# Loading batch 1's tokens and batch 2's x behind batch 0's read, and issuing that read's small moves later

## The chip, the cores and the metric

The kernel runs on one core of one Trainium2 chip. The metric is the device time of one execution, in microseconds. Three executions of the kernel before took 503.93, 504.53 and 505.17 us; the median is 504.53 us.

The engines are named as the profile names them: PE is the matrix engine, with PEld for its weight loads; DVE is the vector engine; ACT is the scalar engine; SP is the engine whose queue issues most of the transfers (SPq in the rows).

## The reference

The program is a two-sided attention between 512 positions and 32 state rows, for 8 batches of 8 heads of width 64, followed by four dense products.

```
scores  = scale * x @ state^T;   a  = softmax(scores);   xread = a  @ state
scores2 = scale * state @ x^T;   a2 = softmax(scores2);  sread = a2 @ x
y   = concat(xread, sread) as (8 * 544) rows of 512
out = ((y @ w1) * (y @ w2)) @ w3 @ w_out
```

All data are float32; the weights come as float64 bits and are converted on the chip.

## The kernel before, in words

**The work per batch.** For each batch b the kernel computes the scores from `x_d` (x with the head's width on the partitions) and `st` (the state), takes both softmaxes, and multiplies the state into w1 and w2 (`sw_steps`), so that the first dense products come straight from the attention weights (`stage1_sums`, line 310). Every float32 operand of a large product is split into a high and a low part (`split`, lines 97 and 98: a copy on ACT, a subtraction on DVE), and three products are summed. Batch 0 is handled by `stage1` and `stage2` in the prologue. Batches 1 to 7 are handled by `quarter_batch`, which does the second dense product in a scheme with fewer multiplications; the combined weights that it needs (`t_parts`) are made by `combine_weights(k)`, k = 0 to 3. The calls with k = 0, 1, 2 stand between batch 0's last pieces, the call with k = 3 stands in batch 1's part, behind its second first-stage piece (lines 497 and 498).

**First-stage pieces.** In `quarter_batch` a loop over ft = 0 to 7 runs 12 large matmuls per piece into a pair of PSUM banks (`two_banks`, three such pairs, named ps). ACT copies one bank (line 484) and DVE multiplies it with the other (line 391); after that the pair is free for a later piece. Behind ft = 1 stand, in this order in the program: the state's read of this batch, the score matmuls of the next batch (line 147), the loads for the batches after, and, in batch 1 alone, `combine_weights(3)`: two sums per call on line 363, four differences on line 369, then a split on lines 97 and 98 named t_hi and t_lo. Then the softmax of the next batch goes on, and the pieces ft = 2 to 7 follow. In `stage2_quarters` two pairs of `sw` products of the next batch (line 147, `units` and `more`) stand between the second-stage products (line 418); they use the same three pairs of banks, and DVE frees a pair with the split named sw_lo.

**The state's read (`read_state`).** It needs two things: the batch's tokens (`x_s`, 1 MB, one buffer only) and the second softmax turned into the tile `a2["t"]`. The second comes from DVE's transpose on line 228 into `blocks` (named work) and 16 transfers of 32 KB that regroup the blocks (`move_blocks`, line 171; for batch 0 the rows read work<-work, for the later batches e<-work). The read is 64 small matmuls (line 243), then on DVE a multiplication (line 248, `scaled`) and a transpose (line 252, `turned`, one buffer only), then 16 transfers of 4 KB that put `turned` into `sread` (line 171, sread<-turned). `sread` is used only at the very end, in `state_rows`.

**What sets the order.** The program order holds on PE and on SP, since both are under `manual_schedule`: what is traced first is issued first. DVE and ACT are ordered, behind the prologue, by a planner that walks through the program with estimated costs, and gives an engine, when it is free, the waiting instruction that stands earliest in the program among those whose inputs it takes to be ready; `high_priority` puts line 391's multiplications first. `side_steps` builds the list of pieces that run between batch 0's last products: first three steps of batch 1's softmax, then batch 0's read and two `sw` products, later the rest of batch 1's softmax (`rest`, with line 228 and its 16 transfers), then two more `sw` products.

**The order on SP around the change.** Before: batch 0's 16 sread<-turned transfers, batch 1's 16 e<-work transfers, then, behind the loop over `tt`, `load_tokens(1)` (x_s of batch 1) and `load_x(2)` (st and x_d of batch 2). The single buffer of `x_s` comes free when batch 0's read has ended on PE.

Of the kernel before, what the change touches and what calls it, by code (L numbers as in the profile page):

```python
# [39 lines left out]
def attn_bilinear_kernel(  # L40
# [47 lines left out]
    def bank():  # L88
        return ps_o.tile([P, NF], F32, name="ps_o")

    def two_banks():
        return ps_2.tile([P, 2, NF], F32, name="ps_2")

    def split(hi, lo, src):

        return (
            nc.scalar.copy(out=hi, in_=src),  # L97
            nc.vector.tensor_tensor(out=lo, in0=src, in1=hi.bitcast(F32), op=ALU.subtract),  # L98
        )
# [41 lines left out]
    def per_head(ps, b, moving):  # L141


        for j in range(NP):
            for q in range(KT):
                rows = slice(q * D, (q + 1) * D)
                nc.tensor.matmul(  # L147
                    ps[j * NS:(j + 1) * NS, q], sts[b][rows, j], moving(rows, j), start=True, stop=True
                )

    def load_x(b):
        sts[b] = att.tile([P, NP, NS], F32, name="st")
        nc.sync.dma_start(out=sts[b], in_=st[b])
        x_tiles[b] = att.tile([P, NP, S], F32, name="x_d", bufs=1)
        nc.sync.dma_start(out=x_tiles[b], in_=x_d[b])

    def load_tokens(b):
        token_tiles[b] = att.tile([P, NT, H, D], F32, name="x_s", bufs=1)
        nc.sync.dma_start(out=token_tiles[b], in_=x_s[b])
# [4 lines left out]
    def work_tile():  # L164
        return att.tile([P, KT, S], F32, name="work")

    def move_blocks(dest, src):

        for j in range(NP):
            for c in range(P // NS):  # L170
                nc.sync.dma_start(  # L171
                    out=dest(slice(c * NS, (c + 1) * NS), j), in_=src(slice(j * NS, (j + 1) * NS), c)
                )

    def attention_steps(b):
        xd = x_tiles[b]
        a2 = {}

        def scores():

            ps = two_banks()
            per_head(ps, b, lambda rows, j: xd[rows, j])
            yield
            flat = lambda t: t.rearrange("p k s -> p (k s)")

            s1 = work_tile()
            nc.vector.transpose(out=flat(s1), in_=flat(ps))

            m2 = att.tile([P, KT], F32, name="m2")
            nc.vector.tensor_reduce(out=m2, in_=ps, axis=AX.X, op=ALU.max)  # L190
            nc.vector.tensor_scalar_mul(m2, m2, -SCALE)
            e2 = att.tile([P, KT, S], F32, name="e2", bufs=1)
            sum2 = att.tile([P, KT], F32, name="sum2")
            a2["e"], a2["sum"] = e2, sum2
            for kt in range(KT):
                one = slice(kt, kt + 1)
                nc.scalar.activation(
                    out=e2[:, kt], in_=ps[:, kt], func=AF.Exp, bias=m2[:, one], scale=SCALE, accum_out=sum2[:, one]
                )

            J = KT * S // NS
            s1v = flat(s1).rearrange("p (j n) -> p j n", n=NS)
            m1 = att.tile([P, J], F32, name="m1")
            nc.vector.tensor_reduce(out=m1, in_=s1v, axis=AX.X, op=ALU.max)
            nc.vector.tensor_tensor(
                out=s1v, in0=s1v, in1=m1.unsqueeze(2).broadcast_to([P, J, NS]), op=ALU.subtract
            )
            nc.scalar.activation(out=s1, in_=s1, func=AF.Exp, scale=SCALE)
            yield
            nc.vector.tensor_scalar_add(sum2, sum2, 1e-9)  # L210
            nc.vector.reciprocal(out=sum2, in_=sum2)
            sum1 = att.tile([P, J], F32, name="sum1")
            nc.vector.tensor_reduce(out=sum1, in_=s1v, axis=AX.X, op=ALU.add)
            nc.vector.tensor_scalar_add(sum1, sum1, 1e-9)
            nc.vector.reciprocal(out=sum1, in_=sum1)
            nc.vector.tensor_tensor(
                out=s1v, in0=s1v, in1=sum1.unsqueeze(2).broadcast_to([P, J, NS]), op=ALU.mult
            )
            yield
            at = work_tile()  # L220
            nc.vector.transpose(out=flat(at), in_=flat(s1))
            at_tiles[b] = [att.tile([P, KT, S], F32R, name=f"at_{part}", bufs=1) for part in ("hi", "lo")]
            last = split(*at_tiles[b], at)
            yield

            blocks = work_tile()
            with tc.issue_after(last[1].ins):
                nc.vector.transpose(out=flat(blocks), in_=flat(e2))
            a2["t"] = work_tile() if b < PLAIN else att.tile([P, KT, S], F32, name="e2", bufs=1)
            tiles = lambda t: t.rearrange("p k (t m) -> p (k t) m", m=P)  # L230
            move_blocks(lambda its, j: tiles(a2["t"])[its, :, j * NS:(j + 1) * NS],
                        lambda mine, c: tiles(blocks)[mine, :, c * NS:(c + 1) * NS])

        def read_state():

            xs = token_tiles[b]

            ps = (bank() if b else two_banks()[:, 0])[:, :KT * D].rearrange("p (k d) -> p k d", k=KT)
            for kt in range(KT):
                for t in range(NT):  # L240
                    for j in range(NP):
                        mine = slice(j * NS, (j + 1) * NS)
                        nc.tensor.matmul(  # L243
                            ps[mine, kt], a2["t"][:, kt, t * P + j * NS:t * P + (j + 1) * NS],
                            xs[:, t, 2 * j + kt], start=(t == 0), stop=(t == NT - 1),
                        )
            scaled = att.tile([P, KT, D], F32, name="scaled")
            a2["read"] = nc.vector.tensor_tensor(
                out=scaled, in0=ps, in1=a2["sum"].unsqueeze(2).broadcast_to([P, KT, D]), op=ALU.mult
            )  # L250
            turned = att.tile([P, KT, D], F32, name="turned", bufs=1)
            nc.vector.transpose(
                out=turned.rearrange("p k d -> p (k d)"), in_=scaled.rearrange("p k d -> p (k d)")
            )
            move_blocks(lambda its, j: sread[its, j, b * NS:(b + 1) * NS],
                        lambda mine, c: turned.rearrange("p k (c n) -> p (k c) n", n=NS)[mine, c])

        return scores, read_state, a2


# [80 lines left out]
    reads = {}  # L341

    def side_steps():

        scores, reads[1], _ = attention_steps(1)
        w = sw_steps(1)
        softmax = scores()

        def rest():

            with tc.issue_after(stored[0].ins):
                yield from softmax

        return [[partial(islice, softmax, 3)], [reads[0], w[0], w[1]], [], [rest], [w[2], w[3]], []]

    QF = FT // 2
    HT, HO = S // 2, DO // 2
# [14 lines left out]
    def tmp_tile():  # L372
        return main.tile([P, NF], F32, name="tmp", bufs=4)
# [102 lines left out]
    def quarter_batch(b):  # L476
        q = {"raw": []}
        w = sw_steps(b + 1) if b + 1 < B else [lambda: None] * 4
        softmax = iter(())
        for ft in range(FT):  # L480
            ps = stage1_sums(b, ft)
            a_sb = tmp_tile()
            with tc.high_priority():
                nc.scalar.copy(out=a_sb, in_=ps[:, 0])  # L484
            hidden_quarters(a_sb, ps[:, 1], ft, q)
            if ft == 1:
                reads[b]()
                if b + 1 < B:
                    scores, reads[b + 1], _ = attention_steps(b + 1)
                    softmax = scores()  # L490
                    next(softmax)
                    load_tokens(b + 1)
                if b + 2 < B:
                    load_x(b + 2)
            elif ft in (2, 4):
                next(softmax, None)
            if b == PLAIN and ft == 1:
                combine_weights(QF - 1)
        stage2_quarters(b, q, w[:2], [*w[2:], lambda: softmax])

    def run(steps):
        for step in steps:
            for _ in step() or ():
                pass


    with tc.tile_pool(name="pro", bufs=2) as pro:
# [62 lines left out]
        softmax = scores()  # L570
# [48 lines left out]
    for tt in range(NT):  # L619
# [5 lines left out]
        run(side[tt])  # L625
        if tt + 1 < QF:
            combine_weights(tt)
    load_tokens(1)
    load_x(2)

    def state_rows():
        n = B * NS
# [26 lines left out]
    for b in range(PLAIN, B):  # L659
        quarter_batch(b)  # L660
# [46 lines left out]
```

## Time and profile before

| what | value |
|---|---|
| executions shown | 503.93, 504.53, 505.17 us; median 504.53 us |
| the profiled execution's own time | 504.66 us |
| its span, first to last instruction | 502.9 us (1.76 us lie around it) |
| PE busy | 488.3 us, 97% |
| DVE busy | 376.8 us, 75% |
| ACT busy | 239.1 us, 48% |
| mean granted PE clock | 0.992 |
| transfers | 52.50 MB, 104 GB/s over the span |

The span begins at 0; all times within it are microseconds from there. A row of the timeline gives start, duration, engine, line, operation, the tiles it writes and reads, and a count; in square brackets stands how long the engine was idle before it, and what ended that. A row of the waits gives engine, tile and line, what it waited for, the total, how often, and the longest. Rows with SPq are the issue of transfers, not their run: the landing comes later. A row of the stretches gives a stretch's limits and length, the busy time of each engine with its number of instructions, the granted PE clock, and the share and rate of the transfers. PE is busy nearly throughout, so its few idle places and the places with a low clock are what to look at first.

### The profile page before, as it was taken

The numbers are of one execution on the slowest core, as the hardware profiler recorded it, in microseconds if no ns is written. First come the engines' busy times: TensorE is split into PE (matmuls) and PEld (weight loads), VectorE is DVE, ScalarE is ACT, GpSimd is POOL, SyncE is SP. The second block draws the span as 40 slices with busy tenths as digits, with TensorE's granted clock in tenths as the row PEclk, the third lists the DMA queues.
The fourth block names the chain that finished last, engine by engine and source line by source line (L and its number), as shares of the span: only waits on it lengthen the run. The fifth ranks groups of instructions, "written<-read, shape, count | busy, mean of one in ns | idle before, by whom it ended". The sixth has DMA issues, their size and how long they took to land.

```text
span 502.9 us, 8937 instructions
## 1 busy us (share of the span) xinstructions
PE 488.3 (97%) x3558; PEld 379.5 (75%) x3558; DVE 376.8 (75%) x555; ACT 239.1 (48%) x364; POOL 0.2 (0%) x4
## 2 busy tenths in 40 slices
PE   8999999999489999999999999999999999999996
PEld 6444467767377988797879787978797889899885
DVE  5769896798499749965995699479937993577770
ACT  4776884354146415722571258135714560354651
POOL 0000000000000000000000000000000000000000
PEclk9999999999799999999999999999999999999999
DMA  8994962013522321331224132404130213001101
GB/s 341 384 422 177 366 243 33 10 47 79 182 89 89 62 66 31 148 82 47 88 93 95 33 113 74 100 23 175 25 103 5 88 43 84 6 3 43 43 2 42
DMA packets 56362, 52.50 MB, mean 104 GB/s; under 512 B 42752, under 2 KB 50944, under 8 KB 51712
## 3 DMA queue, kind: packets, MB, share of 16 engines
q1 hardware_dynamic: 47488, 43.27, 25.9%
q10 hardware_dynamic: 8832, 8.65, 5.0%
q8 instruction: 28, 0.46, 0.4%
q14 instruction: 14, 0.11, 0.1%
HBM read 38.27 MB, written 8.91 MB: 94 GB/s over the span
## 4 chain that ended last, share of the span: by engine, by line
PE 78%; DVE 8%; SPq 6%; ACT 4%; DMA 2%; issue 1%; DVEq 0%; ACTq 0%
PE ps L310 29%; PE ps_o L418 24%; SPq L171 6%; PE ps L147 5%; PE ps L418 4%; PE ps L646 3%; PE ps_o L525 3%; PE ps L525 3%; PE ps_o L324 3%; PE ps_o L243 2%; PE ps L647 2%; DVE w_sb L134 1%; DMA x_s<-in_x_s_dram 1%; ACT ulps L126 1%; DMA raw<-in_w_k_dram 1%
## 5 line engine op out<-in xcount | busy, mean ns | idle before, releaser
L310 PE MATMUL ps<-at_lo,sw_hi 128*128 128x512 f32 x256 | 101.7, 397 | 1.6 <-DVE g_x L391 1.6
L310 PE MATMUL ps<-at_hi,sw_hi 128*128 128x512 f32 x256 | 99.8, 390 | 0.0
L310 PE MATMUL ps<-at_hi,sw_lo 128*128 128x512 f32 x256 | 99.6, 389 | 0.0
L484 ACT COPY tmp<-ps 128x512 f32<-128x512 f32 x56 | 32.8, 586 | 123.6 <-PE ps L310 70.1
L310 PEld LDWEIGHTS ps<-at_lo,sw_hi 128*128 128x128 f32 x256 | 48.1, 188 | 20.1 <-DVE g_x L391 8.2
L310 PEld LDWEIGHTS ps<-at_hi,sw_lo 128*128 128x128 f32 x256 | 48.1, 188 | 10.2
L310 PEld LDWEIGHTS ps<-at_hi,sw_hi 128*128 128x128 f32 x256 | 48.1, 188 | 9.5 <-issue 0.2
L391 DVE TENSOR_TENSOR g_x<-tmp,ps 128x512 f32<-128x512 f32 x28 | 19.1, 684 | 33.5 <-ACT tmp L484 32.9
L98 DVE TENSOR_TENSOR sw_lo<-ps,sw_hi 128x1024 fp32r<-128x1024 f32 (+1 forms) x34 | 37.8, 1151 | 0.2 <-ACT sw_hi L97 0.2
L97 ACT CAST g_hi<-g_x 128x512 fp32r<-128x512 f32 x42 | 26.1, 621 | 20.9 <-PE ps_o L418 14.3
L418 PE MATMUL ps_o<-t_lo,g_hi 128*128 128x256 f32 x168 | 34.5, 287 | 0.0
L418 PE MATMUL ps_o<-wo_lo,g_hi 128*128 128x256 f32 x168 | 34.4, 286 | 0.0
L98 DVE TENSOR_TENSOR g_lo<-raw,g_hi 128x512 fp32r<-128x512 f32 x42 | 28.6, 687 | 7.0 <-ACT g_hi L97 6.3
L418 PE MATMUL ps_o<-wo_hi,g_hi 128*128 128x256 f32 x168 | 33.8, 283 | 0.0
L418 PE MATMUL ps_o<-t_hi,g_hi 128*128 128x256 f32 x168 | 33.8, 283 | 0.0
L418 PE MATMUL ps_o<-wo_hi,g_lo 128*128 128x256 f32 x168 | 33.8, 283 | 0.0
L418 PE MATMUL ps_o<-t_hi,g_lo 128*128 128x256 f32 x168 | 33.8, 283 | 0.0
L97 ACT CAST g_hi<-raw 128x512 fp32r<-128x512 f32 x42 | 25.0, 619 | 17.8 <-DVE raw L391 7.2
L97 ACT CAST sw_hi<-ps 128x1024 fp32r<-128x1024 f32 (+1 forms) x34 | 31.1, 966 | 2.2 <-PE ps L147 2.0
L147 PE MATMUL ps<-w_sb,st 64*32 64x512 f32 (+1 forms) x544 | 31.4, 570 | 0.0
L418 PEld LDWEIGHTS ps_o<-wo_lo,g_hi 128*128 128x128 f32 x168 | 26.6, 191 | 5.6 <-ACT tmp L443 5.0
L418 PEld LDWEIGHTS ps_o<-t_lo,g_hi 128*128 128x128 f32 x168 | 26.1, 192 | 5.0 <-issue 5.0
(109 smaller groups left out, 898.6 us busy)
## 6 DMA issues: line engine op xcount, KB each, us to landing
raw<-in_w_k_dram SPq DMA_DIRECT2D x8, 1024.0 KB, 6.5
x_d<-in_x_d_dram SPq DMA_DIRECT2D x8, 1024.0 KB, 6.9
raw<-in_w_dram SPq DMA_DIRECT2D x8, 1024.0 KB, 6.1
x_s<-in_x_s_dram SPq DMA_DIRECT2D x8, 1024.0 KB, 5.0
out_dram<-tmp ACTq DMA_DIRECT2D x56, 128.0 KB, 1.8
raw<-in_w3t_dram SPq DMA_DIRECT2D x4, 1024.0 KB, 5.2
e<-work SPq DMA_DIRECT2D x112, 32.0 KB, 2.0
sread<-turned SPq DMA_DIRECT2D x128, 4.0 KB, 1.7
```

What stands on the lines that cost most here:

```text
L97: nc.scalar.copy(out=hi, in_=src),
L98: nc.vector.tensor_tensor(out=lo, in0=src, in1=hi.bitcast(F32), op=ALU.subtract),
L147: nc.tensor.matmul(ps[j * NS:(j + 1) * NS, q], sts[b][rows, j], moving(rows, j), start=True, stop=True)
L171: nc.sync.dma_start(out=dest(slice(c * NS, (c + 1) * NS), j), in_=src(slice(j * NS, (j + 1) * NS), c))
L243: nc.tensor.matmul(ps[mine, kt], a2["t"][:, kt, t * P + j * NS:t * P + (j + 1) * NS], xs[:, t, 2 * j + kt], start=(t == 0), stop=(t == NT ...
L310: nc.tensor.matmul(ps[:, i], w[:, kt, c:c + P], a[:, kt], start=(k == 0), stop=(k == 3 * KT - 1))
L324: nc.tensor.matmul(ps[:, :DO], g, wo[w][:, ft, :], start=(ft == 0 and k == 0), stop=(ft == FT - 1 and k == 2))
L391: nc.vector.tensor_tensor(out=whole, in0=a, in1=b, op=ALU.mult)
L418: nc.tensor.matmul(ps[:, tt * HO:(tt + 1) * HO], g[:, tt * P:(tt + 1) * P], w(part, k), start=(fresh and k == 0 and n == 0 and tt == 0), s ...
L484: nc.scalar.copy(out=a_sb, in_=ps[:, 0])
L525: nc.tensor.matmul(w34_ps[i][:, :DO], chunks[k][:, DO + i * P:DO + (i + 1) * P], w_out[k], start=(k == 0), stop=(k == FT - 1),)
L646: nc.tensor.matmul(ps[:, i], wh[:, ks], sr[:, kt], start=(kt == 0), stop=False)
```

## The change

Batch 0's read is cut in two. Its matmuls, `scaled` and `turned` stay where they were; its 16 sread<-turned transfers go behind the 16 e<-work transfers of batch 1. The loads of batch 1's tokens and of batch 2's st and x_d, which stood behind the loop over `tt`, are issued right behind the first half of the read. In `quarter_batch` the read is a generator now and is run to its end at its old place, with its transfers.

```
@@ -252,6 +252,7 @@
             nc.vector.transpose(
                 out=turned.rearrange("p k d -> p (k d)"), in_=scaled.rearrange("p k d -> p (k d)")
             )
+            yield
             move_blocks(lambda its, j: sread[its, j, b * NS:(b + 1) * NS],
                         lambda mine, c: turned.rearrange("p k (c n) -> p (k c) n", n=NS)[mine, c])
 
@@ -344,14 +345,16 @@
 
         scores, reads[1], _ = attention_steps(1)
         w = sw_steps(1)
-        softmax = scores()
+        softmax, read = scores(), reads[0]()
 
         def rest():
 
             with tc.issue_after(stored[0].ins):
                 yield from softmax
-
-        return [[partial(islice, softmax, 3)], [reads[0], w[0], w[1]], [], [rest], [w[2], w[3]], []]
+            yield from read
+
+        loads = [partial(load_tokens, 1), partial(load_x, 2)]
+        return [[partial(islice, softmax, 3)], [partial(islice, read, 1), *loads, w[0], w[1]], [], [rest], [w[2], w[3]], []]
 
     QF = FT // 2
     HT, HO = S // 2, DO // 2
@@ -484,7 +487,7 @@
                 nc.scalar.copy(out=a_sb, in_=ps[:, 0])
             hidden_quarters(a_sb, ps[:, 1], ft, q)
             if ft == 1:
-                reads[b]()
+                run([reads[b]])
                 if b + 1 < B:
                     scores, reads[b + 1], _ = attention_steps(b + 1)
                     softmax = scores()
@@ -625,8 +628,6 @@
         run(side[tt])
         if tt + 1 < QF:
             combine_weights(tt)
-    load_tokens(1)
-    load_x(2)
 
     def state_rows():
         n = B * NS
```

The order on SP becomes: x_s of batch 1, st and x_d of batch 2, batch 1's 16 e<-work transfers, batch 0's 16 sread<-turned transfers, and then batch 1's own sread<-turned transfers as before.

More of the change, by code (lines that the diff above doesn't have):

```diff
@@ L254, in read_state @@
             )
+            yield
             move_blocks(lambda its, j: sread[its, j, b * NS:(b + 1) * NS],
@@ L346, in side_steps @@
         w = sw_steps(1)
-        softmax = scores()
+        softmax, read = scores(), reads[0]()
         def rest():
@@ L352, in rest @@
                 yield from softmax
-        return [[partial(islice, softmax, 3)], [reads[0], w[0], w[1]], [], [rest], [w[2], w[3]], []]
+            yield from read
+        loads = [partial(load_tokens, 1), partial(load_x, 2)]
+        return [[partial(islice, softmax, 3)], [partial(islice, read, 1), *loads, w[0], w[1]], [], [rest], [w[2], w[3]], []]
     QF = FT // 2
@@ L486, in quarter_batch @@
             if ft == 1:
-                reads[b]()
+                run([reads[b]])
                 if b + 1 < B:
@@ L627, in attn_bilinear_kernel @@
             combine_weights(tt)
-    load_tokens(1)
-    load_x(2)
     def state_rows():
```

## The prediction

> **What bounds the kernel now.** I read the page's busy shares first: PE is busy 97% of the span, so the end moves only with PE's idle places and with its clock. The view of waits, for PE, lists all of its idle time; there is one long wait.
>
> ```profile
> PE 488.3 (97%) x3558; PEld 379.5 (75%) x3558; DVE 376.8 (75%) x555; ACT 239.1 (48%) x364; POOL 0.2 (0%) x4
> ```
>
> ```profile
> PE ps_o L243 <- DMA x_s<-in_x_s_dram: 6.9, 1, 6.9
> PE ps L310 <- DVE g_x L391: 1.6, 1, 1.6
> ```
>
> It is batch 1's read, which waits for that batch's tokens. The timeline of PE there, and after it the chain of waits for batch 2, where the same work runs without a wait:
>
> ```profile
> 132.38 2.48 PE L243 MATMUL ps_o<-x_s,e 128*32 128x64 f32 x64 [6.93 <-DMA x_s<-in_x_s_dram]
> ...
> 134.93 1.66 PE L147 MATMUL ps<-x_d,st 64*32 64x512 f32 x16
> ...
> 136.52 0.50 PE L310 MATMUL ps<-at_lo,sw_hi 128*128 128x512 f32 x1
> ...
> 143.82 0.50 PE L310 MATMUL ps<-at_lo,sw_hi 128*128 128x512 f32 x1 [1.56 <-DVE g_x L391]
> ```
>
> ```profile
> 184.75 1.03 PE ps_o L243 x64
> 185.78 1.02 PE ps L147 x16
> 186.80 16.83 PE ps L310 x72
> ```
>
> PE stands from 125.45 (132.38 less 6.93). Read and scores then take 4.14 us (132.38 to 136.52), against 2.05 in batch 2: 2.09 more. The view of stretches says why; the granted clock was halved while PE stood, and came back only at about 135.6:
>
> ```profile
> 127.40:128.40 1.00, 0.00 (x0) 0.00 (x0) 1.00 (x3) 0.66 (x2) 0.00 (x0) 1.00 0.31 33
> ...
> 129.40:130.40 1.00, 0.00 (x0) 0.00 (x0) 0.00 (x0) 0.00 (x0) 0.00 (x0) 0.50 0.96 401
> ...
> 135.40:136.40 1.00, 1.00 (x16) 0.00 (x0) 1.00 (x4) 0.00 (x0) 0.00 (x0) 0.62 0.07 16
> ```
>
> With 1.56 us before the fifth first-stage piece (ft = 4, at 143.82) this place loses 6.93 + 2.09 + 1.56 = 10.6 us. That is all that PE alone could gain. Why the tokens come late is in the timeline of SP's queue:
>
> ```profile
> 77.81 11.44 SPq L171 DMA_DIRECT2D work<-work  x16
> 104.74 10.08 SPq L171 DMA_DIRECT2D sread<-turned  x16
> 114.94 11.54 SPq L171 DMA_DIRECT2D e<-work  x16
> 126.58 0.54 SPq L159 DMA_DIRECT2D x_s<-in_x_s_dram  x1
> ...
> 127.64 0.43 SPq L155 DMA_DIRECT2D x_d<-in_x_d_dram  x1
> ...
> 136.03 10.46 SPq L171 DMA_DIRECT2D sread<-turned  x16
> ```
>
> Some 0.65 us pass per small transfer, so 32 of them hold the loads back from 104.7 to 126.6, though the buffer of x_s is free when batch 0's read ends.
>
> **The loads.** They move up to that read's end. Its rows, with the page's landing times:
>
> ```profile
> 101.10 1.10 PE L243 MATMUL ps<-x_s,work 128*32 128x64 f32 x64
> ```
>
> ```profile
> x_d<-in_x_d_dram SPq DMA_DIRECT2D x8, 1024.0 KB, 6.9
> x_s<-in_x_s_dram SPq DMA_DIRECT2D x8, 1024.0 KB, 5.0
> ...
> e<-work SPq DMA_DIRECT2D x112, 32.0 KB, 2.0
> ...
> sread<-turned SPq DMA_DIRECT2D x128, 4.0 KB, 1.7
> ```
>
> Three issues of about 0.5 us each from 102.2 on, into a queue that is empty between 89.3 and 104.7; x_s lands at about 107.5, x_d at about 110.5, both 15 us before PE wants them. This costs nothing; the cover is that empty queue. The wait of 6.93 us is gone, and the clock's 2.09 us with it.
>
> **The transfers of e.** They no longer stand behind the read's 16. They start when DVE's transpose on line 228 is done, in DVE's rows below: 110.55 + 1.23 = 111.8 instead of 114.94. Sixteen take 11.54 us, so the last is issued at 122.7 and lands 2.0 later, at 124.7. The read starts at 125.45: hidden, with 0.7 us of cover. Were they to start at 114.94 as now, they would land at about 128 and PE would wait 2.5 us.
>
> **The read's own transfers.** Here is the price. They go from 104.74 to behind the e transfers: 123.4 to 133.6 (10.1 to 10.5 us for 16), and the last, issued at about 133.1, lands at 134.8. `sread` is wanted only at the end, which hides that. But `turned` has one buffer, and batch 1's transpose into it must wait until those 16 have read it: not before 134.8. Before, it had been free for 20 us. DVE's timeline there, and batch 2's two rows that I compare with:
>
> ```profile
> 110.55 1.23 DVE L228 STREAM_TRANSPOSE work<-e 128x1024 f32<-128x1024 f32 x1
> ...
> 126.10 0.69 DVE L391 TENSOR_TENSOR g_x<-tmp,ps 128x512 f32<-128x512 f32 x1 [1.17 <-ACT tmp L484]
> ...
> 128.63 0.69 DVE L98 TENSOR_TENSOR g_lo<-tmp,g_hi 128x512 fp32r<-128x512 f32 x1
> ...
> 134.89 0.29 DVE L248 TENSOR_TENSOR scaled<-ps_o,sum 128x128 f32<-128x128 f32 x1 [5.57 <-PE ps_o L243]
> 135.10 0.68 DVE L363 TENSOR_TENSOR tmp<-wo_hi,wo_lo 128x512 f32<-128x512 f32 x1
> 135.70 0.30 DVE L252 STREAM_TRANSPOSE turned<-scaled 128x128 f32<-128x128 f32 x1
> 135.93 0.72 DVE L369 TENSOR_TENSOR raw<-tmp 128x256 f32<-128x256 f32 x2
> ...
> 138.56 1.22 DVE L98 TENSOR_TENSOR t_lo<-raw,t_hi 128x1024 fp32r<-128x1024 f32 x1 [1.12 <-ACT t_hi L97]
> ...
> 139.70 1.24 DVE L187 STREAM_TRANSPOSE work<-ps 128x1024 f32<-128x1024 f32 x1
> ...
> 143.09 0.67 DVE L391 TENSOR_TENSOR g_x<-tmp,ps 128x512 f32<-128x512 f32 x1
> ...
> 161.66 2.34 DVE L98 TENSOR_TENSOR sw_lo<-ps,sw_hi 128x1024 fp32r<-128x1024 f32 x2
> ...
> 185.40 0.69 DVE L391 TENSOR_TENSOR g_x<-tmp,ps 128x512 f32<-128x512 f32 x1 [2.03 <-ACT tmp L484]
> ...
> 210.38 2.35 DVE L98 TENSOR_TENSOR sw_lo<-ps,sw_hi 128x1024 fp32r<-128x1024 f32 x2
> ```
>
> The row of `scaled` shows that DVE waits in its order: 5.57 us idle with the second sum of line 363, which needs nothing of the read, behind it. What stands behind a waiting `turned` waits too: the pieces' multiplications of line 391, which give PE its banks back.
>
> **DVE is the next bound.** From ft = 1's multiplication to the first sw_lo DVE needs 185.40 to 210.38 = 25.0 us in batch 2, without a pause to speak of, and 126.10 to 161.66 = 35.6 us in batch 1. The 10.6 us more are 5.57 idle, 1.12 idle before t_lo, and `combine_weights(3)`: two sums of 0.6, four differences from 135.93 to 137.4, a split of 1.14, together 3.85. That work stays. The first sw_lo frees the banks for the fourth sw product, the second half of this row:
>
> ```profile
> 162.74 1.95 PE L147 MATMUL ps<-w_sb,st 64*32 64x512 f32 x32
> ```
>
> So the product starts at 163.7, and its banks are free at 161.66 + 1.17 = 162.8: 0.9 us to spare. Without both idle times DVE frees them at 162.8 - 5.57 - 1.12 = 156.1. PE alone would be there at 125.45 + 2.05 + two pieces of 2.8 (a sixth of 16.83 each) = 133.1 at ft = 4, and 19.9 later (143.82 to 163.7) = 153.0. The later one counts: 156.1 + S, where S is DVE's wait for `turned`. The gain is 163.7 - 156.1 - S = 7.6 - S.
>
> **How long is S?** The trace before has no such wait, so I bound it. Below: nothing, if the planner takes the transfers to last as long as they do and puts other work first; 134.8 - 129.3 = 5.5 us of such work is there (scores' transpose and maxima, the combined weights). Above: as now, only `scaled` and one sum stand ahead, DVE gets there at 129.3 + 0.25 + 0.6 = 130.15, and S = 4.65. Which is nearer? The planner thinks such transfers faster than they are. It put `scaled` ahead of that second sum, so it took x_s, behind 32 transfers, to be there by about 129; the chip was 5.5 us later. And in batch 1's scores it put the transpose, which needs 16 transfers, ahead of the maximum, which does not:
>
> ```profile
> 90.63 1.25 DVE L187 STREAM_TRANSPOSE work<-ps 128x1024 f32<-128x1024 f32 x1 [2.07 <-DMA work<-work]
> 91.81 1.19 DVE L190 TENSOR_REDUCE m<-ps 128x2 f32<-128x1024 f32 x1
> ```
>
> An estimate from these two rows: it will take the 32 transfers to end 3 to 4 us early, at about 131, and will put one sum and line 187 (its scores now come early, as x_d does) ahead of `turned`. DVE is there at 131.3 and S = 3.5. The gain is 7.6 - 3.5 = 4.1 us.
>
> That must agree with PE's banks. Behind `turned` (0.25) come lines 190 and 204 (1.1 each, 90.63 to 91.81 is one such step) and line 391 (0.67): ft = 4 starts at 134.8 + 3.1 = 137.9, 5.9 earlier than now. PE has then stood 4.8 us from 133.1. The clock fell 3.95 us after PE stopped (125.45 to 129.4), so it falls here too and takes up to 2.09: 3.8 to 5.9, no less than the DVE figure but for 0.3. I take 4.0: 504.66 - 4.0 = **500.7 us**; the profiled run's 504.66 is 0.13 above the median of 504.53, which I leave aside.
>
> [...]
>
> **Rivals.** *No wait at `turned`*: the planner's other work fills the time, S = 0, gain 7.6, **497.1 us**. For it: 5.5 us of work are there; against it: the two rows above. Its outer end is PE's own 10.6 us, 494.1, if the combined weights also found a hole. *The new wait eats it*: order as now, S = 4.65, and the 1.12 before t_lo stays, as line 97 can start only behind the differences: gain 1.8, and with part of the clock's 2.09 on PE less: **503.2 us**. For it: the order now; against: line 187 stood behind t_lo only as long as x_d came late (127.64 + 6.9 = 134.5). *Slower*: the whole of `combine_weights(3)` stands between `turned` and ft = 2's multiplication, as now. `turned` then starts at 134.85 instead of 135.70, the multiplication ends 0.85 earlier, ft = 4 starts at 142.97, after 9.9 us of standing. PE then takes the slow clock's 2.09 there: 1.24 us lost, **505.9 us**. It decides from the point at which that multiplication ends later than 143.76 - 2.09 = 141.7.
>
> **How the numbers follow.** Chances: forecast 0.45, no wait 0.27, eaten 0.18, slower 0.10. A measurement of this kernel tells about 0.3%, 1.5 us, from no change. Faster by that: all of the first two and 0.08 of the third, 0.80; slower: 0.08 of the last; within: the other 0.12. The range goes from 496.0, a little beyond the case without a wait, to 504.8; outside are the slower case and the outer end.
>
> **What would show it.** Right: x_s issued at about 102.2; no wait of PE for x_s; e issued at 111.8, sread at 123.4 to 133.6; DVE idle at line 252 until 134.8, ended by a transfer; PE's next wait at ft = 4 or at the sw products, ended by DVE. Wrong: no idle time at line 252 (then nearer to 497), PE waiting for e<-work at the read, ft = 4 starting later than 141.7, or t_lo standing ahead of line 187.

## The result, and the profile after

The changed kernel takes 499.09 us (median of 5 executions, 497.23 to 499.76) against 505.17 us (5 executions, 503.93 to 505.54): a ratio of 0.988, with a 95% interval of 0.986 to 0.990. Its profiled execution took 499.09 us with a span of 497.3 us, 5.6 us less than the span before. The gain is 6.1 us by the medians and 5.6 by the two profiled executions. Forecast were 500.7 us and a gain of 4.0.

The lines of the changed kernel's code lie a little lower: 310, 363, 369, 391, 418 and 484 of before are 311, 366, 372, 394, 421 and 487 here; those up to 252 are the same. PE's waits:

```profile
PE ps L311 <- DVE g_x L394: 3.4, 1, 3.4
PE ps_o L77 <- DVE work L74: 1.0, 1, 1.0
PE ps_o L528 <- DVE w_sb L134: 0.5, 1, 0.5
```

The wait for the tokens is gone; one for DVE stands in its place. SP's timeline shows the new order:

```profile
102.16 0.34 SPq L159 DMA_DIRECT2D x_s<-in_x_s_dram  x1
...
103.02 1.06 SPq L155 DMA_DIRECT2D x_d<-in_x_d_dram  x1
111.75 11.46 SPq L171 DMA_DIRECT2D e<-work  x16
123.26 22.70 SPq L171 DMA_DIRECT2D sread<-turned  x32
```

The last row holds batch 0's 16 small transfers and, behind a pause, batch 1's. PE's timeline at batch 1's read, and the row of the fourth `sw` product (its second half starts at 158.0, at 163.7 before):

```profile
125.27 1.10 PE L243 MATMUL ps_o<-x_s,e 128*32 128x64 f32 x64
126.30 1.09 PE L147 MATMUL ps<-x_d,st 64*32 64x512 f32 x16
...
139.20 0.50 PE L311 MATMUL ps<-at_lo,sw_hi 128*128 128x512 f32 x1 [3.35 <-DVE g_x L394]
...
157.01 1.95 PE L147 MATMUL ps<-w_sb,st 64*32 64x512 f32 x32
```

Read and scores run without a wait and at a granted clock of 1.00 (125 to 127); then PE goes through three pieces (ft = 2, 3, 4) and stands from 135.85 to 139.20, ahead of ft = 5. DVE's timeline has the reason:

```profile
127.33 0.28 DVE L248 TENSOR_TENSOR scaled<-ps_o,sum 128x128 f32<-128x128 f32 x1
...
130.94 1.24 DVE L187 STREAM_TRANSPOSE work<-ps 128x1024 f32<-128x1024 f32 x1
132.11 0.65 DVE L394 TENSOR_TENSOR g_x<-tmp,ps 128x512 f32<-128x512 f32 x1
135.59 0.31 DVE L252 STREAM_TRANSPOSE turned<-scaled 128x128 f32<-128x128 f32 x1 [2.83 <-DMA sread<-turned]
135.82 0.38 DVE L372 TENSOR_TENSOR raw<-tmp,raw 128x256 f32<-128x256 f32 x1
136.13 1.22 DVE L190 TENSOR_REDUCE m<-ps 128x2 f32<-128x1024 f32 x1
137.32 1.23 DVE L98 TENSOR_TENSOR t_lo<-raw,t_hi 128x1024 fp32r<-128x1024 f32 x1
138.46 0.68 DVE L394 TENSOR_TENSOR g_x<-tmp,ps 128x512 f32<-128x512 f32 x1
...
155.36 1.21 DVE L98 TENSOR_TENSOR sw_lo<-ps,sw_hi 128x1024 fp32r<-128x1024 f32 x1
...
158.23 1.23 DVE L221 STREAM_TRANSPOSE work<-work 128x1024 f32<-128x1024 f32 x1
...
160.57 1.23 DVE L98 TENSOR_TENSOR at_lo<-work,at_hi 128x1024 fp32r<-128x1024 f32 x1
```

`turned` stands 2.83 us until batch 0's small transfers have read its only buffer. Three instructions of 2.6 us follow it, and only then comes ft = 3's multiplication, whose banks ft = 5 needs. Behind PE's pause the granted clock is 0.50, by the view of stretches from 139.9 to 143.3 (0.86 over the last stretch is 0.28 us at 0.50), and the chain of waits gives the three pieces of that time:

```profile
139.00:140.00 1.00, 0.80 (x3) 0.70 (x4) 1.00 (x3) 0.82 (x2) 0.00 (x0) 0.94 0.06 8
140.00:141.00 1.00, 1.00 (x4) 0.71 (x3) 1.00 (x3) 1.00 (x4) 0.00 (x0) 0.50 0.05 7
...
143.00:144.00 1.00, 1.00 (x5) 0.80 (x4) 0.28 (x1) 0.17 (x1) 0.00 (x0) 0.86 0.03 4
```

```profile
139.20 10.06 PE ps L311 x36
```

Three pieces take 8.4 us at a clock of 1.00 (half of 16.83 for batch 2's six in the kernel before), so the slow clock cost 1.65. Of the 10.6 us that PE lost here before, 3.35 + 1.65 = 5.0 are still lost, and 5.6 are gained.

### The profile page after: what moved, and what is told of

The parts are those of the page before. It is cut to its first block, busy times and chain, and to the rows that moved or that the text cites. A ratio compares the mean times of both kernels' runs of the same rounds, so it can differ in the third digit from the quotient of the medians.

```text
span 497.3 us, 8933 instructions
## 1 busy us (share of the span) xinstructions
PE 488.3 (98%) x3558; PEld 379.4 (76%) x3558; DVE 376.2 (76%) x555; ACT 238.6 (48%) x364; POOL 0.2 (0%) x4
## 4 chain that ended last, share of the span: by engine, by line
PE 78%; DVE 10%; SPq 6%; ACT 3%; DMA 2%; issue 1%; DVEq 0%; ACTq 0%
PE ps L311 29%; PE ps_o L421 25%; SPq L171 6%; PE ps L147 6%; PE ps L421 4%; PE ps L647 3%; PE ps_o L528 3%; PE ps L528 3%; PE ps_o L325 3%; PE ps L648 2%; DVE w_sb L134 1%; PE ps_o L243 1%; DMA raw<-in_w_k_dram 1%; DVE sw_lo L98 1%; DVE w_sb L130 1%
```

## The experiments

Each edit is against the changed kernel. Theory A holds that the loss that is left is the wait of `turned`; its rivals are in the expectations.

**The loads alone.**

```
 def rest():
             ...
-            yield from read
...
-        return [..., [partial(islice, read, 1), *loads, w[0], w[1]], ...]
+        return [..., [partial(islice, read, 1), *loads, lambda: read, w[0], w[1]], ...]
```

> The loads alone: x_s, st and x_d are issued behind batch 0's read, but the read's 16 small transfers stay ahead of batch 1's 16 e transfers, as in the kernel before. Theory A (the changed kernel's remaining loss is the wait of batch 1's turned for batch 0's small transfers): turned is free, DVE has no wait at line 252; in its place PE waits at the read for e, which lands at about 128.2 instead of 124.7, so about 2.9 us from 125.3; the time is 504.6 - 10.6 + 2.9 + up to 1.5 = 497 to 498.5, no slower than the changed kernel's 499.1. Theory B (both halves of the change are needed): slower than the changed kernel, 500 to 502.

Measured: 501.94 us, ratio to before 0.995 (0.994 to 0.997), so some 3 us slower than the changed kernel: theory B's figure. Its timeline on SP, SP's waits from 100 to 132, and PE's timeline:

```profile
104.81 13.55 SPq L171 DMA_DIRECT2D sread<-turned  x16
118.48 10.46 SPq L171 DMA_DIRECT2D e<-work  x16
```

```profile
SPq L171 <- DMA x_d<-in_x_d_dram: 2.1, 1, 2.1
SPq L171 <- DMA x_s<-in_x_s_dram: 0.7, 1, 0.7
```

```profile
127.94 0.27 PE L243 MATMUL ps_o<-x_s,e 128*32 128x64 f32 x2 [2.20 <-DMA e<-work]
130.35 1.89 PE L243 MATMUL ps_o<-x_s,e 128*32 128x64 f32 x58 [2.14 <-DMA e<-work]
```

DVE has no wait at `turned` here, as expected. But the small transfers, issued straight behind the big loads, waited 2.8 us in all for these to land, took 13.55 us instead of 10.08, and pushed the e transfers from 114.9 to 118.5. PE waited 4.3 us for e, and not 2.9, and the clock fell as well (0.991 over the span): the last 58 small matmuls took 1.89 us, where all 64 take 1.10 in the changed kernel at a clock of 1.00, and the first matmuls of the next piece start 0.43 us apart until 135.5, 0.23 from 135.8 on. So the second half of the change is worth some 3 us on top of the first, which alone gains 2.5 (501.94 against 504.43 for the kernel before, measured beside it).

**The small transfers alone.**

```
-        return [..., [partial(islice, read, 1), *loads, w[0], w[1]], ...]
+        return [..., [partial(islice, read, 1), w[0], w[1]], ...]
 behind the loop over tt:
+    load_tokens(1)
+    load_x(2)
```

> The second half alone: batch 0's small transfers go behind batch 1's e transfers, the loads stay behind the loop over tt. The 32 transfers then start at 111.8 instead of 104.7 and x_s is issued at about 133.5 instead of 126.6. Theory A: PE waits about 13.4 us at batch 1's read instead of 6.9, and the time is 504.6 + 7 = about 511.5. Theory B (where the small transfers stand matters little by itself): 504 to 506.

Measured: 510.07 us, ratio 1.011 (1.009 to 1.012). On SP and on PE:

```profile
133.03 0.52 SPq L159 DMA_DIRECT2D x_s<-in_x_s_dram  x1
```

```profile
138.35 2.47 PE L243 MATMUL ps_o<-x_s,e 128*32 128x64 f32 x64 [13.22 <-DMA x_s<-in_x_s_dram]
```

PE's wait for the tokens is 13.2 us, as theory A has it. Alone, the second half costs 5.6 us, since it starts the 32 transfers that stand ahead of the loads 7 us later. The halves don't add: alone the loads gain 2.5 us and the small transfers lose 5.6, and together they gain 5.6 to 6.1. The small transfers' new place pays only with the loads moved.

**Two buffers for `turned`.**

```
-            scaled = att.tile([P, KT, D], F32, name="scaled")
+            scaled = att.tile([P, KT, D], F32, name="scaled", bufs=1)
-            turned = att.tile([P, KT, D], F32, name="turned", bufs=1)
+            turned = att.tile([P, KT, D], F32, name="turned", bufs=2)
```

> The changed kernel with two buffers for turned and one for scaled (the room is the same). Batch 1's turned no longer waits for batch 0's small transfers; nothing else moves on DVE but turned itself, to its place behind the g_lo splits. Theory A: DVE's 2.8 us at line 252 and most of PE's 3.35 us before the sixth first-stage piece go, and with them the halved clock behind it (about 1.5 us): 494.5 to 495.5. Theory B (DVE's own work for the combined weights is the bound, and the wait lies in its shadow): 497.5 to 499.

Measured: 494.47 us, ratio to before 0.980 (0.978 to 0.981): 4.6 us less than the changed kernel and the fastest of all. On DVE only `turned` has another place, and it has no wait; on PE the pause has all but gone:

```profile
128.84 0.30 DVE L252 STREAM_TRANSPOSE turned<-scaled 128x128 f32<-128x128 f32 x1
```

```profile
136.39 0.50 PE L311 MATMUL ps<-at_lo,sw_hi 128*128 128x512 f32 x1 [0.26 <-DVE g_x L394]
```

The granted clock is 1.0 in this execution, and 0.999 to 1.0 in all four. This is theory A, and it comes within 0.4 us of the 494.1 at which the prediction put PE alone.

**The combined weights earlier.**

```
-        if tt + 1 < QF:
-            combine_weights(tt)
+        combine_weights(tt)
-            if b == PLAIN and ft == 1:
-                combine_weights(QF - 1)
```

> The changed kernel with combine_weights(3) issued behind batch 0's last piece instead of behind batch 1's second piece: 3.85 us of DVE work leave the stretch with the wait. Theory A: turned still waits until 135.5, the wait grows from 2.8 to about 4 us, the piece behind it gets its banks at about 138.8 as now, and the time stays at 498 to 500. Theory B (DVE's work is the bound): about 3 us faster, 495 to 496.5.

Measured: 496.44 us, ratio 0.984 (0.983 to 0.985), 2.6 us less than the changed kernel. Theory A had expected no change and is wrong on this; the time is in theory B's range, which has DVE's work as the bound. On DVE and on PE:

```profile
134.00 0.68 DVE L394 TENSOR_TENSOR g_x<-tmp,ps 128x512 f32<-128x512 f32 x1
135.65 0.31 DVE L252 STREAM_TRANSPOSE turned<-scaled 128x128 f32<-128x128 f32 x1 [0.96 <-DMA sread<-turned]
```

```profile
134.74 0.50 PE L311 MATMUL ps<-at_lo,sw_hi 128*128 128x512 f32 x1 [1.30 <-DVE g_x L394]
...
155.39 1.09 PE L147 MATMUL ps<-w_sb,st 64*32 64x512 f32 x16 [0.56 <-DVE sw_lo L98]
```

`turned` still starts at 135.65, when the transfers let it, but the planner had other work for DVE ahead of it, and the wait is 0.96. PE's pause is another one now: 1.30 us at ft = 4, for ft = 2's multiplication, which ends at 134.7 ahead of `turned`; then 0.56 us at the fourth `sw` product, for sw_lo. What counts is DVE's wait and its work together: with less of either, PE waits less, here 1.9 us in two places instead of 3.35 in one, and its clock stays at 0.998 to 1.0 in the four executions.

**Both of the last two.**

> Two buffers for turned (one for scaled) and combine_weights(3) behind batch 0's last piece, both. Theory C (the wait at turned and the combined weights' 3.85 us use up the same slack of DVE, so that taking either away takes nearly all of PE's pause): no faster than with two buffers alone, 494 to 495.5. Theory D (each costs its own share): 2 us faster than with two buffers alone, 491.5 to 493.

Measured: 495.55 us, ratio 0.982 (0.981 to 0.984): theory C, and even 1.1 us slower than two buffers alone. Here the rows of DVE and PE are

```profile
127.93 1.23 DVE L98 TENSOR_TENSOR t_lo<-raw,t_hi 128x1024 fp32r<-128x1024 f32 x1 [1.11 <-ACT t_hi L97]
129.07 0.68 DVE L394 TENSOR_TENSOR g_x<-tmp,ps 128x512 f32<-128x512 f32 x1
...
134.14 0.67 DVE L394 TENSOR_TENSOR g_x<-tmp,ps 128x512 f32<-128x512 f32 x1
```

```profile
134.87 0.50 PE L311 MATMUL ps<-at_lo,sw_hi 128*128 128x512 f32 x1 [1.58 <-DVE g_x L394]
```

Put ahead of batch 1, the combined weights hold up ft = 1's multiplication to 129.07 (126.00 in the changed kernel) and all that stands behind it. Ft = 2's multiplication comes at 134.14 (132.41 with two buffers alone), and PE waits 1.58 us for that one at ft = 4. Wait and weights used up the same slack; with the wait gone, the weights stand better where they were.

**The small transfers twice.**

```
-            move_blocks(lambda its, j: sread[...], ...)
+            for _ in range(2 if b == 0 else 1):
+                move_blocks(lambda its, j: sread[...], ...)
```

> The changed kernel with batch 0's 16 small transfers issued twice, the second set writing the same bytes again: turned comes free about 10 us later, at about 145.7. Theory A1 (the wait is as long as the transfers run past the place of the program): the wait grows by 10 us, PE's pause too, 508 to 511. Theory A2 (the planner knows of the transfers and puts other work ahead; the wait is only the part by which it takes them to be faster than they are, some 0.1 us each): turned stands some twelve instructions later on DVE, the wait stays at 2 to 5 us, and the time at 497 to 501.

Measured: 499.97 us, ratio 0.991 (0.989 to 0.992), 0.9 us more than the changed kernel: theory A2. `turned` starts 10.2 us later and waits only 2 us longer:

```profile
145.79 0.31 DVE L252 STREAM_TRANSPOSE turned<-scaled 128x128 f32<-128x128 f32 x1 [4.81 <-DMA sread<-turned]
```

```profile
157.16 1.96 PE L147 MATMUL ps<-w_sb,st 64*32 64x512 f32 x16 [3.45 <-DVE sw_lo L98]
```

The planner moved it behind eleven more instructions, three of the pieces' multiplications among them. So the wait is not the length of the transfers: by where it puts `turned`, the planner knows of them and takes them to be faster than they are. An estimate from these two runs alone puts its error at (4.81 - 2.83) / 16 = 0.12 us for each transfer; that this error makes up the whole wait is not shown. PE now waits at the fourth `sw` product for sw_lo.

**Matmuls of no use in PE's pause.**

```
+            if b == PLAIN and ft == 5:
+                idle, (hi, _) = bank(), at_tiles[b]
+                for n in range(12):
+                    nc.tensor.matmul(idle, sw_tiles[b][0, 0][0][:, 0, :P], hi[:, 0], start=True, stop=True)
             ps = stage1_sums(b, ft)
```

> The changed kernel with 12 matmuls of no use (128x512, 0.23 us each, 2.7 us together, into a bank of their own) ahead of batch 1's sixth first-stage piece, where PE stands for 3.35 us. They fit into the pause. Theory E (the pause itself costs 3.35 us, and the halved clock behind it another 1.5): the pause stays, the clock doesn't fall, 497.2 to 498 in every execution, with a clock of 1.0. Theory F (the slow clock lies in the shadow of DVE's work): 499 to 499.5, as without them.

Measured: 498.82 us, ratio 0.989 (0.987 to 0.990), with clocks of 0.999 to 1.0: about as without them, though the clock no longer fell, and in neither theory's range. On PE and on DVE:

```profile
135.52 2.88 PE L487 MATMUL ps_o<-at_hi,sw_hi 128*128 128x512 f32 x12
...
138.61 0.50 PE L311 MATMUL ps<-at_lo,sw_hi 128*128 128x512 f32 x1 [0.21 <-DVE g_x L394]
...
157.51 1.09 PE L147 MATMUL ps<-w_sb,st 64*32 64x512 f32 x16 [1.60 <-DVE sw_lo L98]
```

```profile
155.10 1.22 DVE L98 TENSOR_TENSOR at_lo<-work,at_hi 128x1024 fp32r<-128x1024 f32 x1
156.24 2.35 DVE L98 TENSOR_TENSOR sw_lo<-ps,sw_hi 128x1024 fp32r<-128x1024 f32 x2
```

This doesn't settle it. With the 12 matmuls in the program the planner put at_lo ahead of sw_lo, so that PE lost 1.60 us at the fourth `sw` product in place of the slow clock.

**The changed kernel's spread.** In the changed kernel's first profile PE's pause ahead of ft = 5 is 3.35 us.

> The changed kernel itself, for the spread of its executions. [...] Theory E (the halved clock behind the pause costs time of its own): the executions with a mean clock of 1.0 lie at about 497.2, those with 0.997 at 499 to 499.3, those with 0.991 at 499.8 or more. Theory F (it lies in the shadow of DVE's work): the time doesn't follow the clock, all lie within 0.5 us.

Measured: 498.62, 498.67 and 499.00 us with a clock of 0.997, and 499.84 with 0.992, which was the profiled one. With the first five executions there are nine of the same program: 497.23 us with a clock of 1.0, six of 498.62 to 499.25 with 0.997, and two of 499.76 and 499.84 with 0.991 and 0.992. The time follows the clock, as theory E has it; but none of the four new executions ran at 1.0, so that its shortest time stands on one execution. In the profile of the one at 499.84, the stretches and the chain of waits:

```profile
138.00:139.00 1.00, 0.15 (x1) 0.15 (x1) 1.00 (x4) 0.17 (x1) 0.00 (x0) 0.55 0.06 8
139.00:140.00 1.00, 1.00 (x3) 0.81 (x4) 1.00 (x2) 1.00 (x3) 0.00 (x0) 0.50 0.05 7
...
143.00:144.00 1.00, 1.00 (x4) 0.81 (x3) 0.00 (x0) 0.00 (x0) 0.00 (x0) 0.50 0.06 8
```

```profile
138.85 11.28 PE ps L311 x36
```

The same three pieces take 11.28 us, 2.9 more than the 8.4 at a clock of 1.00, after a pause of 3.10 us. The clock fell at 138.1 (0.55 over the first stretch), while PE still stood, and was back at 144.9 (0.54 over 144 to 145).

## Why the prediction was right

**The loads.** Right in every term: issued from 102.16 on, no wait for x_s, the clock's 2.09 us at the read gone. The second experiment shows that what stands ahead of the loads sets that wait.

**The transfers of e.** Right: 111.75 to 123.2, and no wait at the read. What it means to lose that cover the first experiment shows: 4.3 us of waiting, where the prediction had 2.5 for a start at 114.94, because the start was later still, at 118.5.

**The new wait.** Right in place and cause, and the third experiment shows it: with a second buffer 4.6 us go. Foretold were a release of the buffer at 134.8 and S = 3.5; measured were 135.6 (one of the 16 issues took 1.55 us instead of 0.6) and 2.83. S is shorter, as the planner put more work ahead: both sums, three of the four differences, line 187 and ft = 2's multiplication. That S hangs on the planner's order and not on the transfers' length was an estimate from two rows; the doubled transfers show it.

**Where PE stands.** The prediction had ft = 4 waiting for ft = 2's multiplication behind `turned`, 4.8 us, then 2.09 us of slow clock at most: 6.9 of the 10.6. With that multiplication ahead of `turned`, PE got one piece further and stood ahead of ft = 5 for 3.35 us; the clock took 1.65. This is the mis-sized term: 5.0 instead of 6.9.

**DVE as the next bound.** This step gave the sum of 4.1, and it failed for this kernel. It took DVE's order from ft = 1 to the first sw_lo as before, so that the fourth `sw` product would come at 156.1 + S, or 158.9 with the S that was measured. The planner changed that order: sw_lo stands ahead of line 221 and at_lo (2.3 us of work), and its banks were free at 155.36 + 1.21 = 156.6, 1.4 us before PE was there at 158.0. The 2.3 us are just the difference between 158.9 and 156.6, so DVE's bound was off by the order alone. What set the time was PE's own path, 153.0 + 3.35 + 1.65 = 158.0. That the bound lies close the other runs show: PE waited there 3.45 us with the transfers doubled, 1.60 with the added matmuls and 0.56 with the combined weights earlier.

So the forecast came near for the right reason, a wait at `turned` that gives back part of the 10.6 us, but its figure owes something to luck: the 4.0 stands between DVE's 4.1, a bound that did not bind, and the 3.8 at PE's low end, which was 1.8 us too little.

**The clock.** The prediction let the slow clock be paid after every pause of 3.95 us or more, by this trace's one row. In the changed kernel's second profile PE stood for 3.10 us only, and the clock fell 2.35 us after it had stopped (135.75 to 138.1); and one execution of nine, at 497.23 us with a clock of 1.0, didn't pay. The prediction also read the clock of before as back at 135.6; its row, 0.62 over 135.40 to 136.40, puts this at 136.2, so that the slow stretch lasted 6.8 us. In the changed kernel it lasted 3.4 us in the first profile and 6.8 in the second.

**The rivals.** The case without a wait, 497.1 us, was 2.0 us from the measured time, the forecast 1.6; the second buffer, which makes that case, gave 494.5, PE's own bound rather than DVE's, since there too sw_lo stands ahead of line 221. The case in which the wait eats the gain needed the 1.12 us ahead of t_lo to stay; t_lo starts at 137.32 without a wait. The slower case needed t_lo ahead of ft = 2's multiplication; the planner put it behind.

## What to carry to other kernels

When a transfer is put behind others on its queue, look not only at who reads what it writes but at who next writes what it reads: with one buffer that writer waited 2.83 us here, and with it all that stood behind it on its engine. A second buffer was worth nearly as much here as the change itself, and shrinking a tile that needs no second copy paid for it. Where a planner orders the engine, such a wait hangs on what it puts ahead (2.83 us in the changed kernel, 0.96 with the combined weights earlier, 4.81 behind twice the transfers), so its order around the place has to be forecast as well as the durations.

## What the runs showed of the hardware that was not expected

By the rows of the stretches, the clock stood at 0.50 for 3.4 us in the changed kernel's first profile (139.9 to 143.3), for 6.8 in its second (138.1 to 144.9) and for 6.8 in the kernel before (129.4 to 136.2). It fell 2.35 us after PE had stopped in the second profile, 3.95 us after it in the kernel before, and 4.0 us after it in the first profile (139.9), when PE had been running again since 139.20. With the loads alone PE's two pauses, 2.20 and 2.14 us with 0.27 us of matmuls between them, were followed by large matmuls 0.43 us apart until 135.5, against 0.23 from 135.8 on.

In the same program a pause of 3.35 us cost 1.65 us more by the clock and one of 3.10 us cost 2.9 more. The execution with a clock of 1.0 was not profiled; added to its 497.23 us, the two losses give 498.9 and, with the shorter pause, 499.8, where 498.6 to 499.3 and 499.8 were measured. That accounts for the changed kernel's spread of 2.6 us; the kernel with two buffers, whose pause is 0.26 us, spreads over 0.6 us.

With the loads alone, SP held back the small transfers behind 2 MB of loads: it waited 2.1 us for x_d and 0.7 for x_s, though the transfers share no tile with these. The run shows that wait, not what ties the transfers together.
